# One scheduler, new costs: hops, landings and bank delays in the plan of an attention-and-feed-forward kernel, with K and Q on one chain of scales

## The chip, the cores and the metric

The kernel runs on one core of a Trainium2 chip. Five engines work side by side, each through its own list of instructions in order: TensorE (PE, matrix products), VectorE (DVE), ScalarE (ACT), GpSimd (POOL) and SyncE (SP, which here only issues transfers). They wait for each other through semaphores. The metric is the device time of one execution in microseconds (us).

## The reference

Four batches of eight heads, 768 positions, 64 numbers per head. Every position of q and k gets a bucket from the signs of six projections; a score counts only where the buckets of q and k agree. Softmax, the product with v, and then a feed-forward layer with an ELU over the joined heads follow.

```
q_bits = (np.einsum('bhsd,dk->bhsk', q, proj) > 0)      # and k_bits the same; a bucket is the six bits
mask   = q_bucket[:, :, :, None] == k_bucket[:, :, None, :]
scores = np.where(mask, scale * np.matmul(q, k.transpose(0, 1, 3, 2)), -1000000000.0)
attn   = np.exp(scores - scores.max(-1)); attn = attn / (attn.sum(-1) + 1e-09)
x      = np.matmul(attn, v).transpose(0, 2, 1, 3).reshape(B * S, H * D)
h      = x @ w_in                                       # 512 -> 2048
out    = np.where(h > 0.0, h, np.exp(np.minimum(h, 0.0)) - 1.0) @ w_out    # 2048 -> 512
```

## The kernel before, in words

Everything that TensorE multiplies is held as two float16 halves (a high part and a rest), after a scaling by a power of two. In front of each product stand therefore a `hi` on ScalarE and a `lo` on VectorE (the lines 205 and 208 of the helpers `a_scaled` and `v_rest`, whatever the tile).

**The work.** A *pair* is two heads of one batch and one half of the query positions; there are 32 pairs (n = 0 to 31), four to a *chunk*, two chunks to a batch. A pair has six score rows of 128 x 768 (`scores`, L755, tile `ss` or `os`). From each, VectorE takes the maximum while it copies the row out of PSUM (`top`, L769, tile `pt`), ScalarE exponentiates (L792), and `hi` and `lo` write the halves (`hl`). Two rows together are a *duo*; they share the small `duo` tile. A DMA transpose per row (L825, `PT<-hl`) turns the halves; when six have landed, TensorE multiplies them with v in 36 matmuls (`attend`, L846, tile `av`), and the result goes to `x` (L861, L864). The tile PT exists twice, and a pair takes both. `pt` and `hl` share one ring of eight buffers (the pool `pp`, tag "p"), while the plan counts four of each.

**The feed-forward part** of a chunk needs the `x` of its four pairs. It goes through 16 blocks: 12 matmuls into `h` (L913), ELU over ScalarE, GpSimd and VectorE (L929, L933, L936, then `hi` and `lo` of `U`), 9 matmuls into `o` and `o2` (L961). While TensorE works on the blocks of chunk c, the pairs of chunk c + 1 are made.

**Preparing q and k.** K is loaded and squared (ScalarE, `accum_out`), its scale is worked out in five small VectorE instructions (`powers`), then `hi`, `lo` and a transpose give K1; Q likewise gives O1 and O2. For the first four pairs the transposes run on TensorE into PSUM banks (`turn`, L384 and L535, and an eviction on ScalarE), later ones as DMA transposes (L397, L552, L555). Bucket bits come from a product with the prepared projection (`z`, L443, or `zh`, L423). The projection itself is loaded from ScalarE's queue (L246) and prepared in 17 VectorE instructions (`prep_proj`). The weights w_in and w_out arrive in 32 slices (L651), are decoded on ScalarE and VectorE (L668, L672, L676) and scaled and halved; the first feed-forward block comes behind that.

**What sets the order.** All engines' lists are written by one planner, `run_plan`. A job has an engine, planned us, a key, jobs it comes `after` (their end) or `behind` (their start), and buffers it takes and gives (`tokens`). Again and again the planner asks for each engine which ready job could start earliest by its own clock, takes of those within 0.05 us the one with the smallest key, and issues the job with the earliest start of all. The instructions of a job are written into their engines' lists at that moment, also those that go to another engine than the job's own: `prep_proj` is a VectorE job, and its two DMAs go into ScalarE's list. The planned times are used for nothing else; on the chip each list runs as fast as its waits allow.

Of the kernel before, what the change touches and what calls it, by code (L numbers as in the profile page):

```python
# [12 lines left out]
I32 = mybir.dt.int32  # L13
# [22 lines left out]
HOP = 0.06  # L36
LATE = {"PE": 0.17, "ACT": 0.1, "DVE": 0.09, "POOL": 0.1, "SP": 0.0}
LEAD = (6.0, 5.0, 4.0, 3.0)
LEAD0 = (-50.0, -4.0, -1.0, 2.0)
V_LEAD = (8.0, 5.0, 4.0, 1.0)  # L40
V_LEAD0 = (-3.0, -2.0, -1.0, 1.0)
W_KEY = (-1.0, 0.35, 1.0, 4.0, 0.3, 12.0, 0.5)
# [6 lines left out]
def lsh_attention_moe(  # L49
# [45 lines left out]
    class Job:  # L95
        __slots__ = ("unit", "us", "do", "key", "give", "take", "move", "start", "end", "left", "ready", "users", "mark")
# [4 lines left out]
              "kx": 3, "qx": 3, "ksc": 3, "qsc": 3, "sg": 3, "duo": 6, "cs": 2}  # L101
    tokens = {name: [0.0] * n for name, n in tokens.items()}

    def job(unit, us, do, key, after=(), behind=(), take=(), give=(), move=None, mark=False):
        j = Job()
        j.mark = mark
# [12 lines left out]
    def run_plan():  # L119
        free = {u: 0.0 for u in ("PE", "ACT", "DVE", "POOL", "SP")}  # L120
        near = {u: [] for u in free}
        dma = 0.0
        for j in jobs:
            if j.left == 0:
                near[j.unit].append(j)
        n = 0
        slow = True
        front = 0.0
        while n < len(jobs):
# [34 lines left out]
            if j.move is not None:  # L164
                dma = max(dma, t + 0.1) + j.move
                j.end = max(j.end, dma) + 1.5
            for name in j.give:
                tokens[name].append(j.end)
            j.do()
            n += 1  # L170
            for o, whole in j.users:
                o.ready = max(o.ready, j.end + (HOP if o.unit != j.unit else 0.0) if whole else j.start)
                o.left -= 1
                if o.left == 0:
                    near[o.unit].append(o)

# [131 lines left out]
    proj_job = job("DVE", 5.0, prep_proj, -90)  # L308
# [754 lines left out]
```

## Time and profile before

| what | us |
|---|---|
| median of 3 runs (lowest, highest) | 942.89 (942.87, 951.15) |
| the profiled execution | 944.45 |
| its span on the core | 942.7 |
| TensorE busy | 832.9 (88%) |
| VectorE busy | 710.4 (75%) |
| ScalarE busy | 701.7 (74%) |
| GpSimd busy | 122.7 (13%) |
| first feed-forward matmul starts | 157.46 |
| last `attend` starts | 829.67 |

The profiled execution lies 1.6 us above the median, and 1.75 us of its time lie outside the span. Busy time of TensorE includes matmuls at a lower granted clock, which take longer; the mean granted clock over the span is 0.948 of full speed. In rows of the trace, `PE` are matmuls and `PEld` weight loads; a bracket `[2.96 <-DVE pt L769]` is idle time of the engine ahead of the row and what ended it; `SPq` and `ACTq` are transfers being issued by these engines' queues. In rows of waits, the numbers are us in total, times, and the longest.

### The profile page before, as it was taken

Reading aid. Unit: us, or ns where it says so; the run is one execution under the profiler, and the core shown is the slowest. Engines: PE = TensorE matmul, PEld = TensorE weight load, DVE = VectorE, ACT = ScalarE, POOL = GpSimd, SP = SyncE. Lnnn points to the kernel's source line nnn. Section 1 sums busy time; section 2 is a strip of 40 time slices with the busy share of each in tenths; the row PEclk is TensorE's granted clock in tenths of the full one; section 3 lists DMA queues with packets and bytes.
Section 4 is the critical chain, followed back from the end, with each engine's and each line's share of the span. In section 5 each row is a group of like instructions: output and inputs, shape, how many; then the busy total and the mean of one; then the engine's idle time right before and its main releaser. Section 6 shows DMA issues by size and latency. Waiting matters only on the chain.

```text
span 942.7 us, 14818 instructions
## 1 busy us (share of the span) xinstructions
PE 832.9 (88%) x5161; PEld 437.6 (46%) x5161; DVE 710.4 (75%) x1506; ACT 701.7 (74%) x1361; POOL 122.7 (13%) x179
## 2 busy tenths in 40 slices
PE   4775567999899998998998999889998999999996
PEld 2332223554445554444454555445554555555553
DVE  6999998998798877898786897788856784722332
ACT  7888878998788898887877999688856885723332
POOL 1000000111120010110111111111111111211211
PEclk9975667999999999999999999999999999999998
DMA  7689997778989899977858897697648752810000
GB/s 265 169 208 232 230 215 177 119 141 166 159 174 163 170 177 164 218 137 142 155 109 182 172 180 149 138 155 137 126 94 163 141 102 29 174 34 1 34 1 33
DMA packets 391338, 135.11 MB, mean 143 GB/s; under 512 B 368000, under 2 KB 385632, under 8 KB 391264
## 3 DMA queue, kind: packets, MB, share of 16 engines
q1 hardware_dynamic: 389184, 127.88, 67.9%
q0 software_dynamic: 1920, 6.29, 1.9%
q8 instruction: 40, 0.66, 0.3%
q14 instruction: 34, 0.28, 0.1%
q10 hardware_dynamic: 160, 0.00, 0.0%
HBM read 35.65 MB, written 6.29 MB: 44 GB/s over the span
## 4 chain that ended last, share of the span: by engine, by line
PE 40%; DVE 25%; DMA 13%; ACT 12%; issue 7%; POOL 1%; SPq 1%; POOLq 0%; DVEq 0%; ACTq 0%
PE h L913 14%; PE o L961 13%; DMA PT<-hl 10%; DVE pt L769 7%; DVE hl L208 6%; PE av L846 6%; PE ss L755 5%; ACT hl L205 3%; ACT pt L792 3%; DVE W L676 2%; DVE U L936 1%; DVE W L208 1%; POOL U L933 1%; DMA vf<-in_v_dram 1%; PE z L443 1%
## 5 line engine op out<-in xcount | busy, mean ns | idle before, releaser
L913 PE MATMUL h<-x,W 128*128 128x384 f16 x1536 | 282.8, 326 | 0.7 <-DVE U L936 0.7
L961 PE MATMUL o<-W,U 128*128 128x512 f16 x1152 | 281.2, 379 | 0.0
L208 DVE SCALAR_TENSOR_TENSOR hl<-pt,duo,hl 128x768 f16<-128x768 f32 x192 | 194.6, 1014 | 25.1 <-ACT hl L205 23.8
L933 POOL TENSOR_SCALAR U<-U,ch 128x384 f32<-128x384 f32 x128 | 105.7, 826 | 787.1 <-ACT U L929 648.9
L205 ACT ACTIVATE hl<-pt,duo 128x768 f16<-128x768 f32 x192 | 176.9, 925 | 33.3 <-DVE duo L805 16.7
L913 PEld LDWEIGHTS <-W 128*128 128x128 f16 x1536 | 148.4, 97 | 113.9 <-issue 5.9
L792 ACT ACTIVATE pt<-pt,duo,sg 128x768 f32<-128x768 f32 x192 | 195.4, 1018 | 2.0
L769 DVE TENSOR_SCALAR_CACHE_REDUCE pt<-ss 128x768 f32<-128x768 f32 x180 | 170.9, 950 | 25.5 <-PE ss L755 14.2
L755 PE MATMUL ss<-K,O 128*128 128x384 f16 x720 | 156.0, 341 | 37.6 <-DVE pt L769 35.0
L961 PEld LDWEIGHTS <-U 128*128 128x128 f16 x1152 | 110.7, 98 | 119.1 <-issue 5.6
L755 PEld LDWEIGHTS <-O 128*128 128x128 f16 (+1 forms) x768 | 74.2, 102 | 122.0 <-issue 61.0
L936 DVE SCALAR_TENSOR_TENSOR U<-h,U 128x384 f32<-128x384 f32 x128 | 70.8, 553 | 70.3 <-POOL U L933 70.1
L205 ACT ACTIVATE U<-U,ch 128x384 f16<-128x384 f32 x128 | 77.8, 607 | 58.0 <-DVE U L936 57.5
L846 PE MATMUL av<-PT,vhl 128*64 128x384 f16 x1152 | 109.9, 344 | 10.0 <-DMA PT<-hl 8.8
L929 ACT ACTIVATE U<-h,ch 128x384 f32<-128x384 f32 x128 | 73.0, 570 | 59.3 <-PE h L913 58.0
L208 DVE SCALAR_TENSOR_TENSOR U<-U,ch 128x384 f16<-128x384 f32 x128 | 78.6, 614 | 37.6 <-ACT U L205 37.4
L846 PEld LDWEIGHTS <-vhl 128*64 128x64 f16 x1152 | 72.6, 115 | 46.2 <-issue 17.7
L785 ACT ACTIVATE duo<-duo,sg 128x2 f32<-128x2 f32 x96 | 27.7, 289 | 25.7 <-DVE pt L769 25.7
L792 ACT ACTIVATION_READ_ACCUMULATOR pt<-pt,duo,sg 128x1 f32 x192 | 36.0, 188 | 0.0
L864 DVE SCALAR_TENSOR_TENSOR x<-av,x 128x384 f16<-128x384 f32 x32 | 17.7, 554 | 21.4 <-ACT x L861 21.4
L687 PE MATMUL acc<-W 128*128 128x128 bf16 x128 | 16.6, 272 | 18.4 <-DVE W L676 18.4
L443 PE MATMUL z<-O,pjz 128*32 128x384 f16 (+1 forms) x168 | 22.2, 336 | 8.7 <-DMA O<-nat2q 6.5
(125 smaller groups left out, 572.1 us busy)
## 6 DMA issues: line engine op xcount, KB each, us to landing
vf<-in_v_dram SPq DMA_DIRECT2D x16, 384.0 KB
U<-in_moe_w_in_dram SPq DMA_DIRECT2D x12, 512.0 KB
U<-in_moe_w_out_dram SPq DMA_DIRECT2D x12, 512.0 KB
out_dram<-W POOLq DMA_DIRECT2D x24, 256.0 KB, 3.6
qst<-in_q_dram SPq DMA_DIRECT2D x30, 192.0 KB
kst<-in_k_dram SPq DMA_DIRECT2D x14, 384.0 KB
PT<-hl SPq DMA_TRANSPOSE x192
W<-in_moe_w_in_dram SPq DMA_DIRECT2D x4, 512.0 KB
```

Source lines behind the costliest of these rows:

```text
L205: nc.scalar.activation(o, x, AF.Copy, scale=s)
L208: nc.vector.scalar_tensor_tensor(o, x, s, hi, ALU.mult, ALU.subtract)
L443: nc.tensor.matmul(t[u * QD : (u + 1) * QD], pj["z"][:rows, zi, :], flat(st[src])[:rows, u * w : (u + 1) * w], start=n == 0, stop=n == len ...
L755: nc.tensor.matmul(t[:, x, :HALF], st[o][:rows, at, :], kst[kk][:rows, j * NC + x * HC : j * NC + (x + 1) * HC, :].rearrange("p a b -> p ( ...
L769: nc.vector.tensor_scalar(pt.rearrange("p (n e) -> p n e", n=2), box["s", at % 2][:, :, :HALF], CLAMP, None, ALU.max, ALU.max, accum_out=b ...
L792: nc.scalar.activation(pt, pt, AF.Exp, bias=u[:, 2 + i : 3 + i], scale=st["sg"][:, 0:1], accum_out=u[:, 4 + i : 5 + i])
L846: nc.tensor.matmul(av[j * D : (j + 1) * D], vst["v"][p][:, j, c, vx, :], PTs[j][:, :, px, c, :], start=n_ == 0 and c == 0, stop=n_ == 2 an ...
L913: nc.tensor.matmul(box["h"], WH[:, g * KT + t, wx, fc * P : (fc + 1) * P], xs[ns[t]][:, xx, :], start=t == 0 and i == 0, stop=t == KT - 1 ...
L929: nc.scalar.activation(box["e"], box["h"], AF.Exp, scale=css[b][:, 0:1])
L933: nc.gpsimd.tensor_scalar(box["e"], box["e"], css[b][:, 2:3], css[b][:, 3:4], ALU.mult, ALU.add)
L936: nc.vector.scalar_tensor_tensor(box["e"], box["h"], 0.0, box["e"], ALU.max, ALU.min)
L961: nc.tensor.matmul(banks[t][:, :DO], box["g"][:, gx, t * P : (t + 1) * P], WH[:, NSI + 1 + f, wx, :], start=f == 0 and i == 0, stop=f == N ...
```

## The change

The planner's model gets larger and more detailed delays, and the plan's keys and costs are set anew:

- a job on another engine counts as ready 0.20 to 0.37 us after its forerunner by engine (0.06 before), and 1.50 us after a transfer's landing;
- a PSUM bank that is given back can be taken 0.30 or 0.58 us later (`BANK_HOP`; 0 before);
- SP may have eight transfers on their way at most (`LANES`);
- transfers' and scale jobs' planned times, the lead times (`LEAD`, `V_LEAD`, `W_KEY`) and the offsets of the pairs' steps (`OFF`) have other values;
- `prep_proj` has key -45 instead of -90, 2.6 us instead of 5.0, and is ready at 5.0 instead of 0.

K and Q of a pair (or of two pairs) get their scales in one chain (`scale_part`) after both squares are there: one shift, multiplication, reciprocal and multiplication over twice as many columns, and two products `sg` of both exponents. For the second half of a batch, where K is there already, Q has a chain of its own, with the products made per pair. The preparation functions are split up for that (`sums_of`, `scale_part`, `k_split`, `q_split`).

The transposes of pair 0 on TensorE go into the two-bank tiles of the scores (`s` and `o`), all twelve of K into one tile with one eviction, where two banks of the ring `h` and two evictions were used. O2's DMA transpose no longer waits in the plan for O1's landing, only for its start.

```diff
-HOP = 0.06
+HOP = {"PE": 0.25, "ACT": 0.30, "DVE": 0.37, "POOL": 0.30, "SP": 0.20}
+DMA_HOP = 1.50
+LANES = 8
+BANK_HOP = {"s0": 0.58, "s1": 0.58, "h": 0.30, "av": 0.30, "PT": 0.30, "hl": 0.00}
-LEAD = (6.0, 5.0, 4.0, 3.0)
+LEAD = (6.7, 6.4, 4.3, 2.5)
...
-OFF = {"S": -0.9, "M": -0.9, "N": -0.6, "E": -0.6, "R": -0.3, "H": 0.0, "L": 0.0, "A": 0.0}
+OFF = {"S": -1.9, "M": -0.9, "N": -0.8, "E": -0.4, "R": -0.3, "H": -0.2, "L": -1.0, "A": 0.0}
...
+                    if u == "SP" and len(lanes) >= LANES:
+                        t = max(t, lanes[-LANES])
...
-                j.end = max(j.end, dma) + 1.5
+                j.end = max(j.end, dma) + 1.4
+                if j.unit == "SP":
+                    lanes += [j.end] * j.lanes
             for name in j.give:
-                tokens[name].append(j.end)
+                tokens[name].append(j.end + BANK_HOP.get(name, 0.0))
...
-                o.ready = max(o.ready, j.end + (HOP if o.unit != j.unit else 0.0) if whole else j.start)
+                hop = DMA_HOP if j.move is not None else HOP[o.unit] if o.unit != j.unit else 0.0
+                o.ready = max(o.ready, j.end + hop if whole else j.start)
...
-    proj_job = job("DVE", 5.0, prep_proj, -90)
+    proj_job = job("DVE", 2.6, prep_proj, -45)
+    proj_job.ready = 5.0
...
+    def scale_part(b, ns, ps, qsts, kbox, qbox, after, key):
...
+            if both:
+                t = ps_a.tile([P, 512], F32, tag="av", name="sum")[:, :w]
+                top = kbox["mx"].bitcast(BF16).rearrange("p (n t) -> p n t", t=2)[:, :, 1]
+                nc.tensor.matmul(t, ones, top, start=True, stop=True)
+                nc.vector.tensor_scalar(mall[:, w:], t, 4.0, None, ALU.max)
+            nc.vector.tensor_scalar(mall[:, :w], qbox["mx"], 4.0, None, ALU.max)
+            nc.vector.tensor_scalar(
+                ex.bitcast(I32), mall.bitcast(I32), 1, 0x7F800000, ALU.logical_shift_right, ALU.bitwise_and
+            )
+            nc.vector.tensor_scalar(ex, ex, 2.0**64, None, ALU.mult)
+            sc = small.tile([P, 4], F32, tag="qs", name="qs")[:, :n]
+            nc.vector.reciprocal(sc, ex)
+            nc.vector.tensor_scalar(sc, sc, 2.0**QK_TOP, None, ALU.mult)
...
-                t1 = job("SP", 1.25, turn1, ky, after=(j2,), take=("O",), move=1.05)
-                t2 = job("SP", 1.25, turn2, ky, after=(j3, t1), give=st["nat"], move=1.05)
+                t1 = job("SP", 1.4, turn1, ky, after=(j2,), take=("O",), move=1.1)
+                t2 = job("SP", 1.3, turn2, ky, after=(j3,), behind=(t1,), give=st["nat"], move=1.1)
...
-                landed.append(job("SP", 1.3, turn, D0 + d + OFF["L"], after=(l,), behind=landed[-1:],
-                                  take=("PT",) if t == 0 else (), give=("hl",), move=2.1))
+                landed.append(job("SP", 1.68, turn, D0 + d + OFF["L"], after=(l,), behind=landed[-1:],
+                                  take=("PT",) if t == 0 else (), give=("hl",), move=2.2))
```

What the new numbers do to the lists is seen in the order of the instructions. First, ScalarE's list at its very beginning, before; `pf` is the projection, `kst` and `qst` are K and Q of pair 0, `W` holds those of pair 1:

```order
L246 DMA pf<-in_proj_dram 64x6 x2
L239 ACT_TABLE_LOAD
L239 ACTIVATE natk,kx<-kst 128x768
L239 ACTIVATE nat1q,qx<-qst 128x384
L239 ACTIVATE W,kx<-W 128x768
```

and in the changed kernel:

```order
L251 ACT_TABLE_LOAD
L251 ACTIVATE natk,kx<-kst 128x768
L258 DMA pf<-in_proj_dram 64x6 x2
L251 ACTIVATE nat1q,qx<-qst 128x384
L251 ACTIVATE W,kx<-W 128x768
L251 ACTIVATE W,qx<-W 128x384
```

The projection's two transfers have moved from the head of the list to behind the squares of pair 0's K, an instruction that waits for K's load. In VectorE's list the 17 instructions of the projection still stand ahead of everything else.

Second, TensorE's list between the last score row of pair 12 and the first of pair 13, before; of equal rows that follow each other one is shown (two matmuls of each kind in a score row, three of each `o`, `o2` and `h` with one operand):

```order
L755 MATMUL ss_3654<-K2_2138,O2_3111 128x384
L961 LDWEIGHTS U_91
L961 MATMUL o_1646<-W_99,U_91 128x512
L961 MATMUL o2_1647<-W_99,U_91 128x512
L755 LDWEIGHTS O1_3282
L755 MATMUL ss_3675<-K1_2257,O1_3282 128x384
```

and the same place in the changed kernel:

```order
L782 MATMUL ss_3765<-K2_1988,O2_3124 128x384
L988 LDWEIGHTS U_91
L988 MATMUL o2_1661<-W_99,U_91 128x512
L940 LDWEIGHTS W_99
L940 MATMUL h_3782<-x16_1792,W_99 128x384
L940 MATMUL h_3782<-x16_2070,W_99 128x384
L940 MATMUL h_3782<-x16_2382,W_99 128x384
L782 LDWEIGHTS O1_3300
L782 MATMUL ss_3800<-K1_2126,O1_3300 128x384
```

Between these two score rows stood 6 matmuls of the second product; now there are 3 of the second and 9 of the first.

Third, SP's list around the transposes of pair 5's Q, before; `PT<-hl` are score rows, `zb` bucket bits of pair 4:

```order
L552 DMA_TRANSPOSE O1_1365<-nat1q_101 128x6x128
L825 DMA_TRANSPOSE PT_1342<-hl_1301 128x12x128
L458 DMA O2_1173<-zb_1368 12x384 x2
L825 DMA_TRANSPOSE PT_1391<-hl_1319 128x12x128
L555 DMA_TRANSPOSE O2_1366<-nat2q_102 128x6x128
```

and in the changed kernel:

```order
L852 DMA_TRANSPOSE PT_1127<-hl_1181 128x12x128
L852 DMA_TRANSPOSE PT_1127<-hl_1193 128x12x128
L579 DMA_TRANSPOSE O1_1216<-nat1q_101 128x6x128
L582 DMA_TRANSPOSE O2_1217<-nat2q_102 128x6x128
L516 DMA O2_1105<-zb_1200 12x384 x2
```

O2's transpose now follows O1's at once, and the score rows ahead of it go in twos.

More of the change, by code (lines that the diff above doesn't have):

```diff
@@ L95, in lsh_attention_moe @@
     class Job:
-        __slots__ = ("unit", "us", "do", "key", "give", "take", "move", "start", "end", "left", "ready", "users", "mark")
+        __slots__ = ("unit", "us", "do", "key", "give", "take", "move", "start", "end", "left", "ready", "users", "mark", "lanes")
     jobs = []
@@ L122, in run_plan @@
         dma = 0.0
+        lanes = []
         for j in jobs:
@@ L340, in k_part @@
             st["nat"] = nat
-            sums.append(job("ACT", 0.83, sq, keys[1] + 0.01 * i, after=(st["kload"],), behind=sums,
-                            take=nat + (("kx",) if i == 0 else ()), give=nat))
-        def scale():
-            if b not in kexs:
-                kexs[b] = small.tile([P, NP], F32, tag="ke", name="ke", bufs=2)
-            _, sc = powers(box["mx"], w, 4.0, QK_TOP, "k", squares=True, ex=kexs[b][:, ps[0] : ps[0] + w])
-            for n, st in enumerate(sts):
-                st["ksc"] = sc[:, n : n + 1]
@@ L351, in k_part @@
-        made = job("DVE", 0.5, scale, keys[1], after=sums, take=("av", "ksc"), give=("av", "kx"))
-        for st in sts:
-            st["made"] = made
+            l = job("SP", 0.5, load, keys[0] + (0 if isk else 0.005) + 0.01 * i, take=() if own else (which + "st",),
+                    move=1.4 if isk else 0.7)
+            made.append(job("ACT", 0.83 if isk else 0.51, sq, keys[1] + 0.01 * i, after=(l,), behind=made,
+                            take=nat + ((which + "x",) if i == 0 else ()), give=nat))
@@ L354, in k_part, with k_split @@
+    def k_split(b, ps, n0, sgs, keys, early, made):
+        sts = [ks[b, p] for p in ps]
         for i, (p, st, sg) in enumerate(zip(ps, sts, sgs)):
@@ L365, in k_part @@
             j1 = job("ACT", 0.83, hi, ky, after=(made,), take=st["nat"])
-            j2 = job("DVE", 0.93, lo, ky, after=(j1,), give=(() if own else ("kst",)) + (("ksc",) if i == w - 1 else ()))
+            j2 = job("DVE", 0.93, lo, ky, after=(j1,), give=() if own else ("kst",))
+            st["lo"] = j2
             def alloc(st=st):
@@ L521, in q_part @@
             j2 = job("DVE", 0.17, dup, ky, after=(j1,))
-            j3 = job("DVE", 0.53, lo, ky, after=(j1,), give=(() if own else ("qst",)) + (("qsc",) if i == w - 1 else ()))
+            j3 = job("DVE", 0.53, lo, ky, after=(j1,), behind=klos, give=(() if own else ("qst",)) + (("qsc",) if i == w - 1 else ()))
             kz = keys[3] + (1.0 * i if not early else 0.0)
@@ L581, in load @@
                 )
-            l = job("SP", 0.4, load, keys[0] + 0.1 * p, take=("v",), behind=box.get("l", ()) or v_last, move=1.4)
+            l = job("SP", 0.5, load, keys[0] + 0.1 * p, take=("v",), behind=box.get("l", ()) or v_last, move=1.4)
             box["l"] = (l,)
@@ L600, in scale @@
             st["ex"], st["sc"] = powers(m1, 1, 2.0**-34, V_TOP, "v", squares=True)
-        made = job("DVE", 0.9, scale, keys[2], after=sums, take=("av",), give=("av",))
+        made = job("DVE", 1.25, scale, keys[2], after=sums, take=("av",), give=("av",))
         st["made"] = made
@@ L655, in w_part @@
             key = W_KEY[0] + W_KEY[1] * i
-            before = job("SP", 0.35, load, key - W_KEY[2], behind=(before,), take=ring, move=1.85)
+            before = job("SP", 0.45, load, key - W_KEY[2], behind=(before,), take=ring, move=1.7)
             slot = i + (2 if i >= NSI else 1)
```

159 lines of the change are left out of this document (90 added, 69 removed).

## The prediction

> **What bounds the kernel now.** I read the page first, then the busy time by stage, then who TensorE waits for, then single stretches of the timeline.
>
> ```profile
> span 942.7 us, 14818 instructions
> PE 832.9 (88%) x5161; PEld 437.6 (46%) x5161; DVE 710.4 (75%) x1506; ACT 701.7 (74%) x1361; POOL 122.7 (13%) x179
> ```
>
> The stages are cut at the first feed-forward matmul and behind the last pair. Columns: busy us of PE, PEld, DVE, ACT, POOL, then the granted clock and the DMA share.
>
> ```profile
> 0.00:157.50 157.50, 97.68 (x553) 47.00 (x554) 141.61 (x339) 125.93 (x236) 3.22 (x27) 0.74 0.83 215
> 157.50:835.00 677.50, 635.51 (x4077) 338.52 (x4076) 537.97 (x1116) 543.25 (x1073) 99.58 (x121) 0.99 0.78 147
> 835.00:942.70 107.70, 99.73 (x535) 52.06 (x532) 30.81 (x52) 32.51 (x54) 19.91 (x31) 0.97 0.04 15
> ```
>
> Three limits, then. The start (157.5 us) is VectorE's, 141.6 busy; it begins only when the projection is there (5.05, below). The middle is TensorE's: 635.5 of 677.5, while VectorE and ScalarE have 20% to spare. The end is TensorE alone, and the last 8 us are the way out. As lists run in order and the work is the same, the time is the first feed-forward matmul's start, plus TensorE's work from there, plus its idle time, plus those 8 us. What a new order can win in the middle is idle time, and its waits are named:
>
> ```profile
> PE ss L755 <- DVE pt L769: 20.2, 27, 3.0
> PE av L846 <- DMA PT<-hl: 8.8, 5, 3.9
> PE z L443 <- DMA O<-nat2q: 6.5, 3, 2.7
> ...
> PE h L913 <- DVE U L936: 0.7, 1, 0.7
> ```
>
> The seven rows of this answer (those left out are 1.8, 1.7 and 1.1) make 40.8 us. The first row is not what it seems. At its worst place VectorE was itself held up:
>
> ```profile
> 376.66 0.96 DVE L769 TENSOR_SCALAR_CACHE_REDUCE pt<-ss 128x768 f32<-128x768 f32 x1 [2.69 <-DMA PT<-hl]
> 377.68 1.44 PE L755 MATMUL ss<-K,O 128*128 128x384 f16 x4 [2.96 <-DVE pt L769]
> ...
> 355.76 0.82 PE L755 MATMUL ss<-K,O 128*128 128x384 f16 x4 [1.04 <-DVE pt L769]
> ...
> 804.52 0.82 PE L755 MATMUL ss<-K,O 128*128 128x384 f16 x4 [1.04 <-DVE pt L769]
> ...
> 243.60 0.82 PE L755 MATMUL ss<-K,O 128*128 128x384 f16 x4 [1.18 <-DVE pt L769]
> ```
>
> The maximum needs a buffer in the ring that `pt` and `hl` share, and that buffer's transpose was not through. Followed back so, nine of the 27 waits, 12.0 us, begin at a transpose (the first at 355.76, the last at 804.52); the other 18 are 8.2 us, the longest at 243.60. The transposes' side is late by itself:
>
> ```profile
> SPq L825 <- PE av L846: 55.3, 7, 21.4
> DVE pt L769 <- DMA PT<-hl: 10.3, 8, 2.7
> ACT hl L205 <- DMA PT<-hl: 15.1, 12, 4.4
> ```
>
> SP waits for `attend` because a pair fills both PT tiles: the next pair's six transposes can start only when the last pair's `attend` is done.
>
> ```profile
> 486.75 3.12 PE L846 MATMUL av<-PT,vhl 128*64 128x384 f16 x36
> ...
> 692.79 3.12 PE L846 MATMUL av<-PT,vhl 128*64 128x384 f16 x36
> ...
> 714.78 4.77 PE L846 MATMUL av<-PT,vhl 128*64 128x384 f16 x35 [3.86 <-DMA PT<-hl]
> ...
> 509.30 4.79 PE L846 MATMUL av<-PT,vhl 128*64 128x384 f16 x35 [2.15 <-DMA PT<-hl]
> 640.08 7.05 SPq L825 DMA_TRANSPOSE PT<-hl  x4
> ```
>
> From the end of one `attend` to the next that had to wait it is 714.78 - 695.91 = 18.9 and 509.30 - 489.87 = 19.4 us: six issues at 7.05 / 4 = 1.8, the last landing, and other transfers between. About 18 us is what a pair's transposes need.
>
> **The change part by part.** The sum is made against the profiled execution (944.45, span 942.7); the median lies 1.6 lower, and I carry the difference over to it.
>
> *Distance between the attends.* I priced TensorE's list between successive `attend`s with these rows (full clock):
>
> ```profile
> 301.94 1.30 PE o L961 x6
> 303.24 0.70 PE z L443 x6
> ...
> 305.02 0.65 PE ss L755 x4
> ...
> 888.03 1.95 PE h L913 x12
> ```
>
> Before, 17 of the 28 distances after pair 3 are under 18 us, the least 14.2, and what they lack to 18 adds up to 35 us; now 3 are, the least 15.7, and 2.5 us are lacking. So `attend`'s 8.8 us go down to about 0.8: **-8.0** (bounds 0 and -8.8). Of the 12.0 us of score waits behind transposes I take two thirds, **-8.0** (bounds 0 and -12.0): the ring is still shared, and the VectorE work between an `hl` and the next `pt` in its buffer is under 8.3 us in 26 cases, before and now. What is late next, if anything, is VectorE, 79% busy in this stage.
>
> *Distance between the scores.* Between two score rows of the middle stood 2.26 us of TensorE work in the median, 1.62 at the lower quarter, and 71 of 162 had under 2.0; now it is 2.76, 2.27, and 8 of 160. Every wait gets about 0.5 us more work in front of it; of the 8.2 us of plain waits, taken one by one less 0.5, 1.6 stay: **-6.6** (bounds +5, should the maxima come that much later too, and -8.2).
>
> *O2's transposes.* In SP's list O2's transpose follows O1's directly in 21 of 28 cases; before it did in 4, and in the rest other transfers stood between, each of which could be waiting. Of `z`'s 6.5 us I take **-4** (bounds 0, -6.5).
>
> *The clock.* After 3.86 and 2.15 us of waiting the 35 matmuls of `attend` took 4.77 and 4.79 us, against 3.12 for 36 elsewhere. If those waits go, so does this: **-3.4** (bounds 0, -4). The Trainium skill ("TensorE: Matmul & The Clock Gate", "What's actually happening") lets the clock fall only after an idle window of about 3.4 us; by it the wait of 2.15 would have been harmless and the term -1.7. The trace disagrees: the row after 2.15 us is as slow as the other.
>
> *The start.* ScalarE used to send for the projection first; now its list holds it behind the square of K, which has to wait for K.
>
> ```profile
> 0.75 1.19 ACTq L246 DMA_DIRECT2D pf<-in_proj_dram  x2
> ...
> 4.24 0.84 ACT L239 ACTIVATE natk<-kst 128x768 bf16<-128x768 f32 x1 [0.97 <-DMA kst<-in_k_dram]
> ...
> 5.05 0.16 DVE L235 TENSOR_REDUCE pjx<-pf 128x1 f32<-128x6 f32 x1 [5.05 <-DMA pf<-in_proj_dram]
> ...
> 157.45 0.56 DVE L864 SCALAR_TENSOR_TENSOR x<-av,x 128x384 f16<-128x384 f32 x1 [0.79 <-ACT x L861]
> ```
>
> From issue to use it took 5.05 - 0.75 = 4.30 us. Issued at 4.24 to 5.08, it is used at 8.5 to 9.4: VectorE, whose list has the projection in front of all, begins 3.5 to 4.3 us later, and it is the bound up to 157.45. If the small transfer takes as long as a load at that time did (5.34, next row) and counts from its second issue at 5.7, it is 11.0, or 6 us later.
>
> ```profile
> 4.84 5.34 DMA vf<-in_v_dram
> ```
>
> The Trainium skill ("DMA: Bandwidth & Descriptors", "Queues, rings and completion order") says that the DMA engines take turns between queues packet by packet, so that ScalarE's transfer would not stand behind all that SP has sent; by that the term keeps to its lower end. No row here shows it yet.
>
> VectorE's own work up to the fourth `x` changes little:
>
> ```profile
> L208 DVE SCALAR_TENSOR_TENSOR hl<-pt,duo,hl 128x768 f16<-128x768 f32 x192 | 194.6, 1014 | 25.1 <-ACT hl L205 23.8
> L769 DVE TENSOR_SCALAR_CACHE_REDUCE pt<-ss 128x768 f32<-128x768 f32 x180 | 170.9, 950 | 25.5 <-PE ss L755 14.2 <-DMA PT<-hl 10.3
> L208 DVE SCALAR_TENSOR_TENSOR nat2q<-qst,qs,nat1q 128x384 f16<-128x384 f32 x30 | 18.6, 620 | 2.1 <-DMA O<-nat2q 2.1
> ...
> L208 DVE SCALAR_TENSOR_TENSOR W<-W,w1s 128x512 f16<-128x512 f32 x16 | 11.9, 747 | 1.5 <-ACT W L205 1.5
> L514 DVE COPY nat1q<-nat1q 128x384 f16<-128x384 f16 x30 | 8.0, 267 | 1.8 <-ACT nat1q L205 1.6
> ...
> L223 DVE TENSOR_SCALAR qe<-qm 128x1 int32<-128x1 int32 x4 | 0.6, 153 | 0.1
> ```
>
> In the list there stand one maximum (0.95) and one `lo` (1.01) more, two pairs' Q more (2 x 0.89), one weight slice less (0.75), and the common chain saves 12 small instructions (12 x 0.15 = 1.8): +1.2. Start: **+5** (bounds 0, where later idle time takes it up, and +10, where other waits come with it). The banks of pair 0 and the missing eviction lie within this idle time: nothing. The common chain makes K wait for Q's square too; in the start that is there long before the projection, in the middle the preparation runs ahead by a lead of over 6 of the plan's rows: nothing.
>
> *Work moved ahead.* Two score rows and one `z` more stand before the first feed-forward matmul: 2 x 0.65 + 0.70 = **-2**.
>
> Sum: -8 - 8 - 6.6 - 4 - 3.4 + 5 - 2 = -27. Span 915.7, profiled 917.5, median 942.9 - 27 = **916**.
>
> **Rivals.** *All of it (0.12).* With transposes never late, all 40.8 us go but 3, with 4 of clock and 2 of work, and the start's delay is taken up: -44, 899. For it: 2.5 us lacking between the attends. Against: the ring's 26 short distances.
>
> *The waits move (0.16).* The lists are in order, and a wait that goes in one place may come in the next; transposes cost SP and DMA what they did (DMA share 0.78 in the middle). Then only the plain score waits shrink: +5 - 2 - 6.6 = about -4, 939.
>
> *Slower (0.12): the transposes go in twos.* Runs of a single PT transpose in SP's list fall from 43 to 3, runs of two rise from 17 to 35. If first ones wait for their partners and second ones queue behind them, a landing comes 1.8 us (7.05 / 4) later in some 35 cases, 63 us; of the 25.4 us that VectorE and ScalarE wait for such buffers TensorE feels 12.0, or 47%: +30. With +5, -2 and -6.6 that is +26, 969. It decides from about half of that price on, when it eats the 27 us with the start. Against it: runs of four stay at 20, and the longer distances leave the transposes time.
>
> **How the numbers follow.** The forecast has 0.60, by itself 905 to 930. Leaving out a tenth on each side takes the upper end through the case of moved waits and the lower end to the first rival: 899 to 942. A change of under 1% can hardly be told in this kernel. Faster by over 1% (under 933.5): forecast, first rival and a little of the second, 0.73; within 1%: the rest of the second, 0.14; slower: 0.13.
>
> **What would show it.** VectorE's first `pjx` at 8.5 to 9.4; the first feed-forward matmul at about 162; rows `PE av <- DMA PT<-hl` nearly gone, `PE ss <- DVE pt` at 6 us or less, `PE z <- DMA O<-nat2q` at 2 or 3; a middle stage with the clock at 1.00. The forecast is wrong if TensorE's idle time there stays above 30 us, or if the fourth `x` comes after 168.

## The result, and the profile after

| | before | changed |
|---|---|---|
| median us (lowest, highest) | 947.02 (942.87, 951.37) | 905.35 (904.02, 907.75) |
| ratio to before, 95% interval | | 0.956 (0.950 to 0.963) |
| the profiled execution's span | 942.7 | 903.9 |
| first feed-forward matmul | 157.46 | 161.41 |
| last `attend` starts | 829.67 | 823.19 |

The kernel before was run once more beside the changed one, hence its new median. The forecast was 916, in a range of 899 to 942, with 0.73 for faster. The kernel is 4.4% faster: the time lies in the range, 11 us under the forecast, and the span fell by 38.8 us where 27 had been forecast. From the page of the changed kernel:

```profile
span 903.9 us, 14772 instructions
PE 821.7 (91%) x5161; PEld 431.0 (48%) x5161; DVE 704.3 (78%) x1482; ACT 699.1 (77%) x1360; POOL 125.8 (14%) x179
...
PE 67%; DVE 18%; ACT 5%; DMA 5%; issue 4%; POOL 0%; SPq 0%; POOLq 0%; DVEq 0%; ACTq 0%
```

The last row is the chain of work that ended last, by engine. The same row before:

```profile
PE 40%; DVE 25%; DMA 13%; ACT 12%; issue 7%; POOL 1%; SPq 1%; POOLq 0%; DVEq 0%; ACTq 0%
```

The same work now hangs on TensorE for two thirds of the span. By stage, cut at the first feed-forward matmul and at the last `attend` (columns as in the prediction):

```profile
0.00:161.41 161.41, 96.06 (x566) 47.22 (x567) 143.71 (x337) 129.70 (x243) 3.22 (x27) 0.74 0.83 217
161.41:823.19 661.78, 652.82 (x4190) 345.48 (x4188) 538.01 (x1108) 545.69 (x1079) 108.00 (x129) 0.99 0.78 149
823.19:903.90 80.71, 72.79 (x409) 38.26 (x408) 22.57 (x38) 23.69 (x40) 14.60 (x23) 0.98 0.05 20
```

TensorE stands still in the middle for 9.0 us. The waits there:

```profile
DVE pt L796 <- PE ss L782: 54.9, 55, 5.1
...
DVE pt L796 <- DMA PT<-hl: 6.7, 5, 3.5
PE ss L782 <- DVE pt L796: 4.0, 5, 2.1
PE av L873 <- DMA PT<-hl: 3.6, 3, 2.0
...
PE sum L228 <- DVE vx L626: 0.8, 3, 0.3
...
PE h L940 <- DVE U L963: 0.3, 1, 0.3
```

TensorE's rows add up to 8.7 us (40.8 before). ScalarE's row for PT transposes (15.1 before) and `z`'s for O2 (6.5) are gone. The first row is the turn: VectorE's maximum now waits 55 times for TensorE's score row, and TensorE 5 times for a maximum. Before, it was 22 times, against 27 times and 20.2 us on TensorE's side:

```profile
DVE pt L769 <- PE ss L755: 12.9, 22, 1.2
```

The groups of instructions show the same for the whole span. Before, the maximum (L769) had waited 14.2 us for `ss`, and `lo` (L208) 23.8 us for ScalarE. Now:

```profile
L220 DVE SCALAR_TENSOR_TENSOR hl<-pt,duo,hl 128x768 f16<-128x768 f32 x192 | 194.0, 1016 | 10.0 <-ACT hl L217 9.3
...
L796 DVE TENSOR_SCALAR_CACHE_REDUCE pt<-ss 128x768 f32<-128x768 f32 x180 | 170.9, 949 | 62.7 <-PE ss L782 55.6 <-DMA PT<-hl 6.7
```

### The profile page after: what moved, and what is told of

It is laid out like the page before. It is cut to its first block, busy times and chain, and to the rows that moved or that the text cites. A ratio compares the mean times of both kernels' runs of the same rounds, so it can differ in the third digit from the quotient of the medians.

```text
span 903.9 us, 14772 instructions
## 1 busy us (share of the span) xinstructions
PE 821.7 (91%) x5161; PEld 431.0 (48%) x5161; DVE 704.3 (78%) x1482; ACT 699.1 (77%) x1360; POOL 125.8 (14%) x179
## 4 chain that ended last, share of the span: by engine, by line
PE 67%; DVE 18%; ACT 5%; DMA 5%; issue 4%; POOL 0%; SPq 0%; POOLq 0%; DVEq 0%; ACTq 0%
PE h L940 23%; PE o L988 23%; PE ss L782 10%; PE av L873 8%; DVE pt L796 4%; DVE hl L220 4%; DMA PT<-hl 2%; PE z L501 2%; DVE W L220 1%; DVE W L703 1%; ACT pt L819 1%; DVE K L485 1%; DVE W L699 1%; DMA pf<-in_proj_dram 1%; ACT hl L217 1%
## 5 line engine op out<-in xcount | busy, mean ns | idle before, releaser
L960 POOL TENSOR_SCALAR U<-U,ch 128x384 f32<-128x384 f32 x128 | 109.1, 852 | 740.2 <-ACT U L956 673.0
L782 PE MATMUL ss<-K,O 128*128 128x384 f16 x720 | 153.8, 337 | 17.0 <-DVE pt L796 16.7
L220 DVE SCALAR_TENSOR_TENSOR U<-U,ch 128x384 f16<-128x384 f32 x128 | 78.7, 615 | 26.8 <-ACT U L217 26.3
L873 PEld LDWEIGHTS <-vhl 128*64 128x64 f16 x1152 | 66.9, 116 | 45.0 <-issue 12.4
L812 ACT ACTIVATE duo<-duo,sg 128x2 f32<-128x2 f32 x96 | 27.7, 289 | 34.3 <-DVE pt L796 34.2
L714 PE MATMUL acc<-W 128*128 128x128 bf16 x128 | 16.0, 270 | 20.2 <-DVE W L703 20.2
L510 DVE TENSOR_SCALAR zb<-z,pjt 64x384 f16<-64x384 f32 (+1 forms) x40 | 24.1, 602 | 1.8 <-PE z L501 1.8
```

What stands on the lines that cost most here:

```text
L220: nc.vector.scalar_tensor_tensor(o, x, s, hi, ALU.mult, ALU.subtract)
L782: nc.tensor.matmul(t[:, x, :HALF], st[o][:rows, at, :], kst[kk][:rows, j * NC + x * HC : j * NC + (x + 1) * HC, :].rearrange("p a b -> p ( ...
L873: nc.tensor.matmul(av[j * D : (j + 1) * D], vst["v"][p][:, j, c, vx, :], PTs[j][:, :, px, c, :], start=n_ == 0 and c == 0, stop=n_ == 2 an ...
L960: nc.gpsimd.tensor_scalar(box["e"], box["e"], css[b][:, 2:3], css[b][:, 3:4], ALU.mult, ALU.add)
```

## The experiments

The table holds all kernels. "Middle" is TensorE's idle time between the first feed-forward matmul and the last `attend`, by the rows of its waits; "maxima" the part of it that waits for `pt`; "transposes" what VectorE (`pt`), ScalarE (`hl`) and TensorE (`attend`) wait there for PT transposes, three rows added (before: 10.3 + 15.1 + 8.8). "From h on" is the span less the start of the first feed-forward matmul. "Lacking" and "short gaps" are read from the order as in the prediction: us that the attend distances lack to 18, and score gaps with under 2.0 us of TensorE work. Ratios are to the kernel before on the same chip; the half width of their intervals is 0.002 to 0.006, and widest for the changed kernel. Where two variants lie 3 to 6 us apart, their intervals can overlap while their single runs do not; the text says so where much hangs on it. An edit of the planner makes all lists anew. How far two plans differ by accident was not measured, so a few us between two plans are weak evidence that the edit itself is the cause.

| kernel | median | ratio | first h | from h on | middle | maxima | transposes | lacking | short gaps |
|---|---|---|---|---|---|---|---|---|---|
| before | 947.0 | 1 | 157.5 | 785.2 | 40.8 | 20.2 | 34.2 | 35 | 71 |
| changed | 905.4 | 0.956 | 161.4 | 742.5 | 8.7 | 4.0 | 10.3 | 2.5 | 8 |
| changed, no room | 947.0 | 0.999 | 164.8 | 779.3 | 36.5 | 32.0 | 34.6 | 31 | 70 |
| before, with room | 921.7 | 0.972 | 160.7 | 759.8 | 20.7 | 14.7 | 28.5 | 10.5 | 9 |
| before, room and planned transfers | 917.6 | 0.970 | 164.3 | 750.6 | 15.4 | 8.2 | 30.0 | 11 | 5 |
| changed, old keys | 908.1 | 0.958 | 166.6 | 739.0 | 9.1 | 3.9 | 22.4 | 12 | 5 |
| changed, no bank delay | 909.6 | 0.959 | 162.8 | 744.8 | 11.0 | 8.4 | 21.6 | 17 | 63 |
| changed, no landing delay | 919.3 | 0.969 | 162.1 | 754.3 | 18.8 | 8.5 | 22.8 | 16 | 10 |
| changed, no engine hops | 913.3 | 0.966 | 162.4 | 747.8 | 14.7 | 8.8 | 20.3 | 13 | 37 |
| before, two rings | 942.6 | 0.995 | 158.2 | 781.8 | 35.5 | 11.5 | 27.2 | 35 | 71 |
| changed, two rings | 901.8 | 0.951 | 162.2 | 737.6 | 6.5 | 1.4 | 5.9 | 2.5 | 8 |
| changed, projection first | 899.8 | 0.949 | 157.3 | 741.0 | 7.1 | 3.2 | 9.1 | 2.5 | 8 |
| both of these | 897.3 | 0.948 | 157.2 | 736.7 | 6.1 | 1.9 | 4.8 | 2.5 | 8 |
| both, room 1.3 times | 898.6 | 0.950 | 156.0 | 742.0 | 7.2 | 1.0 | 5.0 | 2.9 | 9 |

### Is it the room? All of it out, and all of it alone

Out of the changed kernel:

```diff
-HOP = {"PE": 0.25, "ACT": 0.30, "DVE": 0.37, "POOL": 0.30, "SP": 0.20}
-DMA_HOP = 1.50
-LANES = 8
-BANK_HOP = {"s0": 0.58, "s1": 0.58, "h": 0.30, "av": 0.30, "PT": 0.30, "hl": 0.00}
+HOP = {"PE": 0.06, "ACT": 0.06, "DVE": 0.06, "POOL": 0.06, "SP": 0.06}
+DMA_HOP = 0.06
+LANES = 100000
+BANK_HOP = {}
```

> The changed kernel with all the room taken out of the planner again (a hop of 0.06 us everywhere, no landing or bank delay, no limit on transfers under way), but with its new keys, leads, common scales and banks. In the order, 14 of 28 distances between successive attends are under 18 us and lack 31 us (after: 3 and 2.5; before: 17 and 35), and 70 score gaps have under 2.0 us of TensorE work (after 8, before 72). Theory (the time hangs on these two distances): TensorE's idle time in the middle comes back to 30 to 45 us from 8.8, and the kernel takes 30 to 38 us more than the changed one, 935 to 943. Rival 1 (the new keys and leads carry the gain): within 8 us of the changed kernel, 905 to 913. Rival 2 (half each): about 922.

947.0, as slow as the kernel before (0.999, 0.997 to 1.002): everything else in the change is worth nothing in total by itself. That is a balance of two parts. The first feed-forward matmul comes 7.4 us later than before (the projection, sent for at 7.08 us, is used at 13.16), and from there on the kernel is 5.9 us shorter, 2.0 of it for matmuls moved ahead. The waits of that kernel's middle:

```profile
PE ss L782 <- DVE pt L796: 32.0, 39, 3.1
DVE pt L796 <- DMA PT<-hl: 18.6, 14, 3.1
ACT hl L217 <- DMA PT<-hl: 15.0, 10, 4.1
DVE pt L796 <- PE ss L782: 13.6, 18, 1.2
...
PE z L501 <- DMA O<-nat2q: 1.3, 2, 0.9
PE av L873 <- DMA PT<-hl: 1.0, 1, 1.0
```

The distances lack 31 us, and yet `attend` waits for 1.0 us. The late transposes are there (34.6 us in all), but they hold the buffers of `pt` and `hl`, and TensorE feels them as waits for maxima. The row of `lo` shows VectorE's other side, 48.7 us of waiting for ScalarE, against 9.3 in the changed kernel:

```profile
L220 DVE SCALAR_TENSOR_TENSOR hl<-pt,duo,hl 128x768 f16<-128x768 f32 x192 | 195.1, 1017 | 49.2 <-ACT hl L217 48.7
```

Put into the planner of the kernel before, with nothing else (no `LANES` either):

```diff
-HOP = 0.06
+HOP = {"PE": 0.25, "ACT": 0.30, "DVE": 0.37, "POOL": 0.30, "SP": 0.20}
+DMA_HOP = 1.50
+BANK_HOP = {"s0": 0.58, "s1": 0.58, "h": 0.30, "av": 0.30, "PT": 0.30, "hl": 0.00}
...
-                tokens[name].append(j.end)
+                tokens[name].append(j.end + BANK_HOP.get(name, 0.0))
...
-                o.ready = max(o.ready, j.end + (HOP if o.unit != j.unit else 0.0) if whole else j.start)
+                hop = DMA_HOP if j.move is not None else HOP[o.unit] if o.unit != j.unit else 0.0
+                o.ready = max(o.ready, j.end + hop if whole else j.start)
```

> The kernel before with hops, landing delay and bank delay put into its planner, and nothing else of the change (old keys, scales apart, projection sent for first). In the order, 11 of 28 attend distances are under 18 us and lack 10.5 us; 9 score gaps have under 2.0 us. Theory (distances): score waits and the z waits go as in the changed kernel (about -20), attend's waits go by half (-3), the start keeps its old length: 25 to 35 us under the kernel before, 908 to 918. Rival 1 (keys, leads and common scales carry the gain): within 8 us of the kernel before, 935 to 943. Rival 2 (half each): about 922.

921.7, 25 us less, rival 2 in size; whether the keys are the other half is asked below. The room carries 25 of the 42 us alone, and without it the rest carries nothing in total; the other 17 us are an effect of other edits on a plan that has room.

### Which part of the room?

Each part alone taken out of the changed kernel.

```diff
-BANK_HOP = {"s0": 0.58, "s1": 0.58, "h": 0.30, "av": 0.30, "PT": 0.30, "hl": 0.00}
+BANK_HOP = {}
```

> The changed kernel with the bank delay alone taken out of the planner (a bank given back can be taken at once again). In the order, 63 score gaps of 160 have under 2.0 us of TensorE work (8 with it), and 15 attend distances are under 18 us and lack 17 us (3 and 2.5 with it). If the score gap carries most of the gain: TensorE's waits for the maxima in the middle come back from 4.0 to 20 us or more, and the kernel takes 15 to 25 us more than the changed one, 920 to 930. Rival 1 (the attend distance alone counts): waits of attend and of hl buffers come back, some 10 us, 912 to 918, with TensorE's waits for the maxima under 10. Rival 2 (the hops and landings suffice): within 4 us of the changed kernel.

909.6, between the two rivals. This run takes the score gap out of the theory: 63 gaps are short, nearly as many as in the kernel before, and the cost is 4 us, which the intervals (0.957 to 0.961, and 0.950 to 0.963 for the changed kernel) do not tell from nothing.

```profile
DVE pt L796 <- PE ss L782: 17.1, 30, 1.5
DVE pt L796 <- DMA PT<-hl: 13.2, 16, 1.7
PE ss L782 <- DVE pt L796: 8.4, 16, 1.1
ACT hl L217 <- DMA PT<-hl: 8.4, 10, 1.4
```

I divided the waits for maxima by whether VectorE or ScalarE had waited for a PT transpose in the 5.5 us before. Before, 12.2 us stand behind a transpose and 8.0 do not; here 6.4 and 1.9; with no room at all 21.3 and 10.8. So short gaps cost little where hops and landings have their room.

```diff
-DMA_HOP = 1.50
-LANES = 8
+DMA_HOP = 0.06
+LANES = 100000
```

> The changed kernel with the landing delay back at 0.06 us and no limit on transfers under way; hops and bank delays stay. In the order, the score gaps stay long (10 under 2.0 us, 8 before this edit), but 15 attend distances are under 18 us and lack 16 us (3 and 2.5 before it). If the attend distance has a price of its own: waits of attend, and of VectorE and ScalarE for PT transposes (6.7 us and none in the changed kernel), come back to 15 us or more, and the kernel takes 8 to 16 us more, 913 to 921. Rival 1 (only the score gap counts): within 4 us of the changed kernel, 902 to 909. Rival 2 (late landings upset z and the score rows behind Q's transposes as well): over 20 us more, with z's and the scores' waits for transposes in the list.

919.3, 14 us more, within the 913 to 921 that the first theory gave, with waits for transposes at 22.8 us where it said 15 or more; but `attend`'s own waits are 3.7, no more than in the changed kernel, and `z` waits 3.0 us for O2's transposes again. The limit of eight transfers has no part in this: without it alone, the planner writes the same lists, instruction for instruction.

```diff
-HOP = {"PE": 0.25, "ACT": 0.30, "DVE": 0.37, "POOL": 0.30, "SP": 0.20}
+HOP = {"PE": 0.06, "ACT": 0.06, "DVE": 0.06, "POOL": 0.06, "SP": 0.06}
```

> The changed kernel with the hops between engines back at 0.06 us; landing and bank delays stay. So far the parts of the room, each taken out alone, cost 4 us (bank delay) and 14 us (landing delay; the limit of eight transfers moves no instruction), and all of it together 42 us. In the order, 37 score gaps under 2.0 us, 12 attend distances under 18 us that lack 13 us. Theory A (the parts add up, and the engine hops carry the rest): about 42 - 18 = 24 us more than the changed kernel, 925 to 933. Theory B (the parts stand in for each other, since any of them moves the score rows' forerunners ahead; only all of them gone costs the 42): 4 to 12 us more, 909 to 917. In both, VectorE's waits for ScalarE's hl, 9 us in the changed kernel and 49 with no room at all, grow: over 35 us by A, under 28 by B.

913.3, as theory B had it, with VectorE's waits for ScalarE's `hl` at 26.3 us over the span. The parts, each taken out alone, cost 4 + 14 + 8 = 26 us, all together 42: they stand in for each other. The waits for maxima that are not behind a transpose stay at 1.5 to 3.4 us in all three kernels and come back (10.8) only when the whole room is gone.

### The shared ring

The order unchanged, `pt` and `hl` in two rings of four buffers; first in the kernel before:

```diff
-                    pt = pp.tile([P, S], F32, tag="p", name="pt")
+                    pt = pp.tile([P, S], F32, tag="p", name="pt", bufs=4)
...
-                    hl = pp.tile([P, 2, S], F16, tag="p", name="hl")
+                    hl = pp.tile([P, 2, S], F16, tag="l", name="hl", bufs=4)
```

> The kernel before, its order unchanged, with pt and hl in two rings of four buffers each instead of one ring of eight. It tests the reading that nine of the 27 score waits (12.0 us) came from a maximum that had to wait for a buffer which a late transpose still read. If so, the rows of VectorE waiting for PT transposes ahead of the maximum (10.3 us) vanish, TensorE's waits for it fall from 20.2 to 8 to 12 us, and the kernel is 6 to 12 us faster, 931 to 937. Rival (the wait only moves to ScalarE, which then waits for an hl buffer instead): ScalarE's 15.1 us of such waits grow to about 25, TensorE's waits stay at 17 or more, and the time is within 3 us of the kernel before.

```profile
ACT hl L205 <- DMA PT<-hl: 18.9, 13, 4.9
DVE pt L769 <- PE ss L755: 11.9, 23, 1.4
PE ss L755 <- DVE pt L769: 11.5, 23, 1.4
PE av L846 <- DMA PT<-hl: 8.3, 6, 3.7
```

VectorE's row for transposes is gone and TensorE waits 8.7 us less for maxima, as the reading of the held buffers said. The time fell by only 4.6 us instead of 6 to 12 (ratio 0.995, 0.993 to 0.997): part of the wait moved on to ScalarE, 15.1 to 18.9, and in the middle as a whole 5.3 us are gained. The same edit in the changed kernel:

> The changed kernel, its order unchanged, with pt and hl in two rings of four buffers. In the kernel before this took TensorE's waits for the maxima from 20.2 to 11.5 us and 4.6 us of the time. If what is left of such waits in the changed kernel (4.0 us, behind 6.7 us of VectorE's waits for transposes) has the same cause: VectorE's row vanishes, TensorE's waits for the maxima fall to 1 to 2 us, and the time falls by 1 to 4 us, 901 to 904. Rival (the room already took all that could be had): ScalarE waits for hl buffers instead and the time stays within 1 us.

901.8, 3.5 less (900.3 to 903.4, against 904.0 to 907.8). VectorE's 6.7 us are gone, ScalarE has 2.3, and TensorE waits 1.4 us for maxima. The ring still had a price; the intervals (0.948 to 0.954, and 0.950 to 0.963) overlap, the runs do not.

### The start

The projection's two transfers at the head of ScalarE's list again:

```diff
+        pj["f"] = const.tile([P, NB], F32, name="pf")
+        for j in range(2):
+            nc.scalar.dma_start(pj["f"][j * D : (j + 1) * D, :], proj)
...
-        pf = const.tile([P, NB], F32, name="pf")
-        for j in range(2):
-            nc.scalar.dma_start(pf[j * D : (j + 1) * D, :], proj)
+        pf = pj["f"]
```

> The changed kernel with one thing back: the projection's two transfers stand again at the head of ScalarE's list. The order of all else is the same. If the start term is real and carries through to the end: the first pjx at 5 to 6 us instead of 11.0, the first feed-forward matmul at 156 to 158 instead of 161.4, and 3 to 5 us less in all, 900 to 902. Rival 1 (later idle time took the delay up): the first feed-forward matmul earlier, but the whole within 1.5 us of the changed kernel. Rival 2 (VectorE then waits for K and Q instead): pjx early, and the first feed-forward matmul within 1 us of 161.4.

In the timeline of the changed kernel,

```profile
3.87 0.84 ACT L251 ACTIVATE natk<-kst 128x768 bf16<-128x768 f32 x1 [1.84 <-DMA kst<-in_k_dram]
3.88 1.28 ACTq L258 DMA_DIRECT2D pf<-in_proj_dram  x2
...
11.04 0.16 DVE L247 TENSOR_REDUCE pjx<-pf 128x1 f32<-128x6 f32 x1 [11.04 <-DMA pf<-in_proj_dram]
```

and of this kernel:

```profile
0.75 1.20 ACTq L137 DMA_DIRECT2D pf<-in_proj_dram  x2
...
5.30 0.16 DVE L250 TENSOR_REDUCE pjx<-pf 128x1 f32<-128x6 f32 x1 [5.30 <-DMA pf<-in_proj_dram]
...
157.30 0.95 PE L941 MATMUL h<-x,W 128*128 128x384 f16 x3
```

VectorE begins 5.7 us earlier, the first feed-forward matmul comes 4.1 us earlier, and the time is 5.6 less, 899.8. The start's delay was not taken up by anything later. (The intervals, 0.945 to 0.953 and 0.950 to 0.963, overlap a little; the runs, 899.2 to 900.3 and 904.0 to 907.8, do not.)

### Where the other 17 us come from

All of the changed kernel, but with the old keys, leads and offsets:

```diff
-LEAD = (6.7, 6.4, 4.3, 2.5)
-LEAD0 = (-50.0, -4.4, -2.9, 3.4)
-V_LEAD = (8.3, 4.9, 6.5, 1.9)
-V_LEAD0 = (-1.1, -3.9, -2.4, 0.8)
-W_KEY = (-1.0, 0.32, 1.0, 5.4, 0.30, 12.0, 0.50)
+LEAD = (6.0, 5.0, 4.0, 3.0)
+LEAD0 = (-50.0, -4.0, -1.0, 2.0)
+V_LEAD = (8.0, 5.0, 4.0, 1.0)
+V_LEAD0 = (-3.0, -2.0, -1.0, 1.0)
+W_KEY = (-1.0, 0.35, 1.0, 4.0, 0.3, 12.0, 0.5)
...
-OFF = {"S": -1.9, "M": -0.9, "N": -0.8, "E": -0.4, "R": -0.3, "H": -0.2, "L": -1.0, "A": 0.0}
+OFF = {"S": -0.9, "M": -0.9, "N": -0.6, "E": -0.6, "R": -0.3, "H": 0.0, "L": 0.0, "A": 0.0}
```

> The changed kernel with all the room, but with the keys, leads and offsets of the kernel before (LEAD, LEAD0, V_LEAD, V_LEAD0, W_KEY, OFF). The kernel before with the same room took 25 us less than without; the changed one 42 us less. In the order, 5 score gaps under 2.0 us, 10 attend distances under 18 us that lack 12 us. If the other 17 us come from the keys: 915 to 923, with TensorE's waits in the middle at 15 to 22 us. Rival 1 (they come from the common scales, the banks of pair 0 and the planned times of transfers): within 5 us of the changed kernel, 900 to 910. Rival 2 (half each): about 913.

908.1, rival 1. From the first feed-forward matmul on it is even 3.5 us shorter than the changed kernel (ten more matmuls stand ahead of that point, 1.4 us of it); the new keys are worth 5.2 us in the start, and nothing behind it. In the whole that is 2.7 us, which the intervals do not tell from nothing. So I asked the other way round. The kernel before, with the room and the changed planned times of the transfers (with O2 behind O1's start and the limit of eight transfers), of which these are the main lines:

```diff
-                t1 = job("SP", 1.25, turn1, ky, after=(j2,), take=("O",), move=1.05)
-                t2 = job("SP", 1.25, turn2, ky, after=(j3, t1), give=st["nat"], move=1.05)
+                t1 = job("SP", 1.4, turn1, ky, after=(j2,), take=("O",), move=1.1)
+                t2 = job("SP", 1.3, turn2, ky, after=(j3,), behind=(t1,), give=st["nat"], move=1.1)
...
-                landed.append(job("SP", 1.3, turn, D0 + d + OFF["L"], after=(l,), behind=landed[-1:],
-                                  take=("PT",) if t == 0 else (), give=("hl",), move=2.1))
+                landed.append(job("SP", 1.68, turn, D0 + d + OFF["L"], after=(l,), behind=landed[-1:],
+                                  take=("PT",) if t == 0 else (), give=("hl",), move=2.2))
```

> The kernel before with the room (hops, landing and bank delays) and the changed planned times of all transfers (a PT transpose 1.68 us of SP's list instead of 1.3, O2 behind O1's start, and so on); keys, scales, banks of pair 0 and the projection as before. With the room alone it took 921.7; the changed kernel with its old keys took 908.1 with a start that was 5 us later than the changed kernel's. If the planned times of the transfers are what the room alone lacked: waits in the middle fall from 20.7 to 8 to 12 us, 902 to 910. If the common scales and pair 0's banks are: still 917 to 924, with the waits at 17 or more. Half each: about 912.

917.6, with 15.4 us of waits. By the time that is the second guess, but the waits lie between the two, and the start of this kernel came 3.5 us later than with the room alone. In the whole it is 4.1 us faster than that kernel, and the intervals overlap. From h on it is 750.6, against 759.8: there the planned transfers take 9.2 us off, of which 12 matmuls moved ahead are 2.0. From 750.6 to the 739.0 of the changed kernel with the old keys it is another 11.6 (10 matmuls moved ahead are 1.4 of it). What differs between these two are above all the common chain of scales (24 VectorE instructions less in the page's count, 1506 to 1482) with its own waits and places in the order, pair 0's banks, the planned times of the scale jobs and the projection's key and ready time. Which of them it is was not tried, so this part of the gain has no shown cause.

### Together, and more of it

The changed kernel with the projection first and two rings:

> The changed kernel with the projection sent for first and with pt and hl in two rings. Apart, the two took 5.6 and 3.5 us off. The one is in the start and the other in the middle; if nothing later takes them up they add: 895 to 898. Rival (the earlier middle meets the same landings later, so that one of the two is lost): 899 to 902.

897.3 (895.7 to 898.7), 0.948 of the kernel before (0.944 to 0.953) and 8 us under the changed one; 5.6 and 3.5 add up to 9.1. Against the projection first alone the intervals overlap. And the same with every hop, landing and bank delay 1.3 times as large:

```diff
-HOP = {"PE": 0.25, "ACT": 0.30, "DVE": 0.37, "POOL": 0.30, "SP": 0.20}
-DMA_HOP = 1.50
+HOP = {"PE": 0.325, "ACT": 0.390, "DVE": 0.481, "POOL": 0.390, "SP": 0.260}
+DMA_HOP = 1.95
...
-BANK_HOP = {"s0": 0.58, "s1": 0.58, "h": 0.30, "av": 0.30, "PT": 0.30, "hl": 0.00}
+BANK_HOP = {"s0": 0.754, "s1": 0.754, "h": 0.390, "av": 0.390, "PT": 0.390, "hl": 0.00}
```

> As the kernel with the projection first and two rings, with all hops, landing and bank delays 1.3 times as large. In the order, 9 score gaps under 2.0 us with 2.92 us in the median (2.76), 4 attend distances under 18 us that lack 2.9 (2.5). If the room is used up (waits in the middle are 6 to 7 us by now, part of them a transpose's own length): within 3 us of that kernel, 893 to 900. If more room still pays: 3 us or more under it, with the waits under 4. If more room makes the plan keep instructions back that could go: 3 us or more over it, with a later first feed-forward matmul or new waits for x.

898.6, the same within what can be told; the middle waits 7.2 us where it waited 6.1. By this one step the room is used up.

## Why the prediction was right, and where it was not

**The bound.** TensorE's list with its idle time was the right thing to count. Idle in the middle went from 40.8 to 8.7, -32.1; the terms of the sum that make it up (8 + 8 + 6.6 + 4) were 26.6. The four terms were off by +2.8, -2.1, +0.5 and -2.5, so that they nearly cancel, which is luck. A further 4.2 us lie in rows that the sum had put at nothing: `z` waiting for `x` and for `zb`, `attend` for `zb`, and the like fell from 5.3 to 1.1. Two rivals fell: moved waits would have left the idle time as it was, and transposes in twos would have landed late, but ScalarE's and VectorE's waits for them fell from 25.4 to 6.7.

**Attend, -8.0: mis-sized, and its rule too narrow.** It went from 8.8 to 3.6, -5.2. "What they lack to 18" is not a forecast of `attend`'s own wait (31 lacking and 1.0 us of wait with no room; 16 and 3.7 without landing delay). It goes along with the waits for transposes on all three engines together: 34 us where 31 to 35 are lacking (27 with two rings), 20 to 23 at 12 to 17, 5 to 10 at 2.5 to 3. Two kernels stand outside: those built from the kernel before with room wait 28 and 30 us at 10.5 and 11. Nor do these waits set the time by themselves: they are 22.4 us with the old keys and 22.8 without the landing delay, but TensorE stands still in the middle for 9.1 us in the one and 18.8 in the other.

**Held buffers, -8.0: right.** 12.2 us of such waits became 2.1. The two rings showed by themselves that the held buffers are a cause; they brought 4.6 us in the kernel before and 3.5 in the changed one. The two thirds in the sum were a guess.

**Plain score waits, -6.6: right in size, wrong in reason.** They went from 8.0 to 1.9. The step that failed is "Every wait gets about 0.5 us more work in front of it": without the bank delay the gaps are short again and the plain waits stay at 1.9, and in the kernel before with room the gaps are long and 5.2 us of them stay. All kernels with few of them (0.6 to 3.4 us) have some room in the hops or landings and the changed planned times of the transfers. A likely reason is that the plan then knows how late a row's chain through VectorE and ScalarE is; it was not shown.

**O2's transposes, -4: all 6.5 went, and the reason fell.** I had it from O2 following O1 at once in SP's list. With the room alone O2 follows O1 directly in none of 28 cases, and `z` waits 0.2 us in the middle; without the landing delay it does in 17, and `z` waits 3.0. The waits go with the landing delay: the ten kernels that have it wait 0.2 us or less, the four without it 1.3 to 7.1.

**The clock, -3.4: mis-sized.** In the changed kernel two waits are still followed by slow matmuls:

```profile
278.27 4.76 PE L873 MATMUL av<-PT,vhl 128*64 128x384 f16 x35 [1.99 <-DMA PT<-hl]
```

The granted clock (the third figure from the end) in the four stretches of 4 us of that kernel, between the start and the last matmul, in which it was clearly lowered:

```profile
237.00:241.00 4.00, 2.79 (x10) 1.38 (x10) 3.50 (x8) 2.21 (x3) 0.00 (x0) 0.67 1.10 210
241.00:245.00 4.00, 4.00 (x21) 2.00 (x20) 1.89 (x3) 2.34 (x6) 0.66 (x1) 0.90 0.95 142
277.00:281.00 4.00, 2.73 (x24) 2.20 (x26) 1.71 (x9) 2.00 (x5) 0.00 (x0) 0.79 0.65 138
281.00:285.00 4.00, 4.00 (x26) 2.23 (x22) 1.17 (x3) 0.52 (x2) 0.00 (x0) 0.78 0.37 85
```

That is 4 x (0.33 + 0.10 + 0.21 + 0.22) = 3.4 us lost; before, five such stretches lost 4 x (0.43 + 0.31 + 0.12 + 0.21 + 0.22) = 5.2. So -1.7. The forecast took away all waits of that length, and two were left: this one, and 2.13 us ahead of a score row at 238.21. It had also left out one of the slow stretches before, behind the 2.96 us at 377.68.

**The start, +5: right in size, by another landing.** It was +3.95 at the first feed-forward matmul. The first `pjx` came at 11.04 and not at 8.5 to 9.4: the transfer took 7.16 us from its first issue where 4.30 had been taken from the row at the head of the list. The 11.0 that I had given as the worst case was met by luck, since the issue came earlier (3.88) and the transfer took longer than in that sum; 2 of the 6 us were made up before 161. The Trainium skill's turns between queues ("DMA: Bandwidth & Descriptors", "Queues, rings and completion order") had been taken to keep the term at its lower end; that reading failed, since the small transfer alone on its queue took 7.16 us, more than the load that had been the worst case (5.34). Whether it took turns with SP's loads or stood behind them, no run here shows.

**Work moved ahead, -2: right.** 14 matmuls, two score rows and one `z`, 2.0 us.

**What the sum had no term for.** +3.95 - 32.1 - 1.7 - 2.0 is -32; 7 us of the 38.8 are missing. Most of it is in what the windows call busy: from the first feed-forward matmul on TensorE is busy for 652.82 + 72.79 = 725.6 us, and was for 630.22 + 105.06 = 735.3 before (cut at 157.46 and 829.67). Less the clock and the 14 matmuls, 6 of these 9.7 us are the same matmuls taking less time. The kernel before shows why in its row of `h`:

```profile
L913 PE MATMUL h<-x,W 128*128 128x384 f16 x1536 | 282.8, 326 | 0.7 <-DVE U L936 0.7
```

One of these matmuls is given as 326 ns long, by its modelled end, but twelve in a row take 1.95 us, 0.16 each. The last matmul ahead of a wait therefore counts some 0.16 us too much as busy, and the row of the wait that much too little. TensorE waited 42 times in the middle before and 12 times now, so an estimate from these rows is 30 x 0.16 = 4.9 us. Counted from start to start of the matmuls in both traces, the stretches with a wait are 4.8 us shorter beyond what the rows of waits say. The last 2 us were not traced. With no room the figure is 632.72 + 101.18 = 733.9 again.

## What to carry to other kernels

Where a planner writes the lists of engines that then run in order, the delays it believes in can matter more than its priorities: here all other edits without the delays were worth nothing in total, the delays alone 25 us, and of the three kinds of delay each taken out alone lost 4 to 14 us of the 42. Look at which side of a pair of engines waits: here, once VectorE waited for TensorE and hardly for ScalarE or transposes, 1.3 times the room bought nothing. And when jobs issue transfers into another engine's list, read that list's head: a small load that had moved behind one instruction cost 5.6 us. It was the new ready time of 5.0 that moved it, and not the key: with the old key of -90 the planner writes the same lists, and without the ready time the load stands at the head again.

## What had not been expected of the hardware

A transfer of 64 x 6 numbers, twice, took 4.3 to 5.1 us from its first issue to its use in the seven kernels that issue it at the head of ScalarE's list (0.75 us), and 6.1 to 7.3 us in the seven that issue it at 3.9 to 7.1 us, while SP's loads go on. The size is the same, so it does not explain the difference. What was on its way already is a likely reason, but no run varied that alone.

Waits of about 2 us can be followed by slow matmuls: 35 matmuls of `attend` took 4.76 us behind 1.99 us of waiting in the changed kernel, and 4.79 behind 2.15 in the one before; 36 elsewhere took 3.12. The length of the wait alone does not decide it. In the kernel before, a wait of 2.75 us was not followed by a lower clock; the granted clock from 443 to 447 us was 1.00:

```profile
443.24 0.50 PE L443 MATMUL z<-O,pjz 64*32 64x384 f16 x4 [2.75 <-DMA O<-nat2q]
```

The Trainium skill ("TensorE: Matmul & The Clock Gate", "What's actually happening") speaks of an idle window of about 3.4 us; the slow rows behind 1.99 and 2.15 us do not agree with that.
